# Attention and a gated MLP interleaved on TensorE: every phase takes four score units, and the slots of the other products are spread evenly over the phases

## The chip, the core and the metric

The kernel runs on one core of a Trainium2 chip. The metric is the device time in microseconds (us) of one execution, smaller is better. The times shown of the kernel before are three runs with a median of 1246.99 us (1246.35 to 1248.84).

## The reference, cut to what matters

One input x of 2048 tokens by 512 features goes through two branches, which a gate mixes token by token.

```python
g = sigmoid((x * gate_w).sum(-1, keepdims=True))
# branch A: 32 query heads of 16 features, one shared key head and value head
q = (x @ wq).reshape(B, S, 32, 16).transpose(0, 2, 1, 3)
p = softmax(einsum("bhqd,bkd->bhqk", q, x @ wk) * 16 ** -0.5)
a = einsum("bhqk,bkd->bhqd", p, x @ wv)   # heads side by side, then @ wo
# branch B: 512 -> 1792 -> 512
b = square(relu(x @ w1 + b1)) @ w2 + b2
out = g * a + (1 - g) * b
```

The weights wq and wk are drawn large, so scores are large and the kernel shifts them before the exponential by bounds on the norms of q and k. A second, exact path (`exact_shift`) stands behind a flag at the end and does not run on these inputs.

## The kernel before, in words

**Attention, in score units.** The work of branch A is cut into 32 iterations, each for four heads and 512 queries. An iteration has 16 key tiles of 128 keys, and each key tile is taken for two halves of 256 queries: 32 *score units* in an iteration, 1024 in all (`total`, L1000). `scores` (L723 to L735) makes one unit: two matmuls (L730; one on rows 0 to 63 of the array, one on rows 64 to 127, which run beside each other) fill a PSUM tile `s` of 128 keys by 1024, and ScalarE takes its exponential into `e` in SBUF (L734). The pool of `s` has two buffers (`sp`, L254), so the scores of a unit cannot be written before the exponential of the unit two places earlier has read its buffer. `context` (L737 to L747) multiplies the exponentials by the values: for two units together four matmuls of 512 columns, or for units one by one four of 256 columns (in the last iteration, where `place`, L718, orders the units by halves first), each head on its own 32 columns of the array (L745). The result gathers in `acc`.

**All other products, in slots.** Query projection, both MLP layers and the output projection are one long stream (`stream`, L188; `work`, L942). A product of 128 tokens by 512 has 12 steps or so, three for each 128 deep slice, since numbers are split into a rounded part and a rest. A step that is taken is called a *slot*: a matmul on rows 0 to 63 of the array and the partner, on rows 64 to 127, of a step taken five slots before (`LAG`, L214). So a slot issues two matmuls that run beside each other, or one alone where the stream starts, ends or has to wait for data. The variable `left` (L1001) counts the slots that are still to come; it starts at 1720. When a product is complete, VectorE takes it out of PSUM (L637 to L643 and L664 for the MLP, L239 to L242 and L972 for the output projection). The pool `mp` has three PSUM buffers.

**Phases.** The main loop (L1044 to L1058) works in phases. The order on TensorE is written by hand: `phase` (L1003) issues the scores of the next few units and, between them, slots; after it `context` handles the units of the phase before. In `phase`, the first unit's scores come first, then slots, with a further unit's scores after every third slot if the phase has more than three slots (L1020), and what is left of the units after the last slot (L1022). `plan` (L1030) says how many units and slots a phase takes:

```python
if left > max(total - u - 4, early) and u % FULL == 0:
    return range(u, min(u + FULL, total)), 8
return range(u, min(u + LIGHT, total)), 3 if left > total - u else 2
```

As long as more slots are left than units, a phase takes four units and eight slots; later phases take two units and two or three slots. In the built program that makes 175 phases of four units with eight slots each, and then 162 phases of two units with two slots each (some of these slots issue a single matmul).

**Chores.** Once in each phase `turn_of_chores` (L606) does a small piece of other work: it splits a weight tile, loads something, or splits a piece of the attention's output. It keeps a rough clock of its own, which a phase advances by 4.9 or 2.1 (L609), and a budget that depends on whether the phase has more than three slots. In phases of more than three slots the rounding of weights runs on ScalarE (L1026 to L1028, the copies of L491); in smaller phases VectorE does it (L617). `finish` (L761) copies `acc` out at the end of an iteration, on ScalarE (L771). The query norms (`qnorm`, L427) take one `s` buffer four times in the run, and the pieces of the division by the row sums run one in a phase (`side`, L1011).

**The end.** After the last unit the loop runs one phase without scores, then the last context, and then: what is left of the stream (L1064), the last half of the attention output (`half`, L818, with short filler matmuls, `busy`), and two last products.

Of the kernel before, what the change touches and what calls it, by code (L numbers as in the profile page):

```python
# [22 lines left out]
NC, CH = 4, 512  # L23
NG = 8
NK = S // 128
NF = F // 128
# [9 lines left out]
PARTS = [slice(a, min(a + 86, CH)) for a in range(0, CH, 86)]  # L36
LANDS = 8.0
GROUPS = (0, 1, 2, 3), (4, 5, 6, 7), (8, 9, 10), (11, 12, 13)
FULL, LIGHT = 4, 2
LAG = 5  # L40
HC = CH // 2

# [107 lines left out]
def mix_kernel(ctx: ExitStack, tc: tile.TileContext, xT, wkv, wq, wo, w12, b1, b2, cst, out):  # L150
# [37 lines left out]
    def stream(units, pp):  # L188

        late = []

        def follow(keep):
            if len(late) > keep:
                late.pop(0)()

        for unit in units:
            if unit is None:
                if late:  # L200
                    follow(0)
                    yield 1
                else:
                    yield 0
                continue
            terms, outs, tag = unit
            banks = [pp.tile([128, CH], F32, name=tag)]

            def product(i, half, terms=terms, outs=outs, banks=banks, tag=tag):
                if len(banks) == half:  # L210
                    banks.append(pp.tile([128, CH], F32, name=tag))
                a, b = terms[i]
                rows = slice(64 * half, 64 * half + 64)
                nc.tensor.matmul(banks[half], a[rows], b[rows], start=i == 0, stop=i == len(terms) - 1)  # L214
                if i == len(terms) - 1:
                    outs[half](banks[half])

            for i in range(len(terms)):
                late.append(lambda i=i, p=product: p(i, 1))
                product(i, 0)  # L220
                follow(LAG)
                yield 1
        while late:
            follow(0)
            yield 1
# [27 lines left out]
    with fast, tc.tile_pool(name="at", bufs=1) as at, \  # L253
# [207 lines left out]
        clock = 0.0  # L461
# [22 lines left out]
        def w_rest(half):  # L484
            n = len(ws[half])
            r, l = ws[half][n] = rounded[half][n]
            nc.vector.tensor_tensor(l, wf[half][n], r.bitcast(F32), OP.subtract)  # L487
            wanted.append(half)
# [4 lines left out]
        def w_split(half):  # L493
            if len(rounded[half]) == len(ws[half]):
                w_round(half, nc.vector.tensor_copy)
            w_rest(half)

        def w_ready(half):
            n = len(rounded[half])
            return (n == len(ws[half]) and n in since[half] and n < min(room[half], NC * NF)  # L500
                    and clock - since[half][n] > LANDS)
# [104 lines left out]
        def turn_of_chores(slots):  # L606

            nonlocal clock, held
            clock += 4.9 if slots > 3 else 2.1  # L609
            if soon:  # L610
                return soon.pop(0)()
            spare = (BUDGET if slots > 3 else BUDGET - 0.3) - (1.2 if side else 0.0)
            for half in halves():
                if len(rounded[half]) > len(ws[half]):
                    w_rest(half)
                    spare -= 0.7
                elif slots < 4 and spare > 1.0 and w_ready(half):  # L617
                    w_split(half)
                    spare -= 1.1
            if spare > 1.0 and chores and clock > held:  # L620
                if chores.pop(0)():
                    held = clock + 6.0

        def halves():
            return (0, 1) if len(ws[0]) < begun[0] + 2 else (1, 0)
# [371 lines left out]
            return pairs(r[:, cols], l[:, cols], wos[0][:, t], wos[1][:, t])  # L997

        side, lazy = [], stream(work(), mp)
        total, early = NC * NG * 2 * NK, 4 * 9 + 6  # L1000
        left = 12 * (15 + NC * NF * 2 + 3 * 4) + early + 2 * LAG  # L1001

        def phase(us, slots):  # L1003

            nonlocal left
            us = list(us)
            if ripe:
                qnorm(ripe.pop(0))
            ripe.extend(narrow)
            narrow.clear()  # L1010
            if side and next(side[0], "end") == "end":  # L1011
                side.pop(0)
            turn_of_chores(slots)
            if us:
                scores(us.pop(0))
            for i in range(1, slots + 1):
                if not next(lazy, None):
                    break
                left -= 1
                if i % 3 == 0 and us and slots > 3:  # L1020
                    scores(us.pop(0))
            for u in us:  # L1022
                scores(u)
            while wanted:
                w_load(wanted.pop(0))
            for half in halves():  # L1026
                if slots > 3 and not soon and w_ready(half):
                    w_round(half, scalar_copy)  # L1028

        def plan(u):  # L1030


            if left > max(total - u - 4, early) and u % FULL == 0:
                return range(u, min(u + FULL, total)), 8
            return range(u, min(u + LIGHT, total)), 3 if left > total - u else 2

        acc, us = None, ()
        nxt, slots = plan(0)
        phase(nxt, slots)
        v_tiles(range(9, 16), vp)  # L1040
# [3 lines left out]
        while us:  # L1044
            it, k = divmod(us[0], 2 * NK)
            if k == 0 and it + 1 < NC * NG:
                q_load(it + 1)
            nxt, slots = plan(us[-1] + 1)
            phase(nxt, slots)
            if k == 0:  # L1050
                acc = ap.tile([128, CH], F32, name="acc")
            context(acc, us)
            if us[-1] % (2 * NK) == 2 * NK - 1 and it < NC * NG - 1:
                finish(it, acc)
            if us[-1] == total - NK - 1:
                side.append(half(acc, 0))
                next(side[-1])
            us = nxt  # L1058
# [51 lines left out]
```

## Time and profile before

| what | value |
|---|---|
| median of three runs | 1246.99 us |
| span of the profiled execution, first to last instruction | 1243.9 us |
| what lies around the span (median less span) | 3.1 us |
| TensorE (PE) matmuls busy | 1233.2 us, 99% of the span |
| ScalarE (ACT) busy | 1060.3 us, 85% |
| VectorE (DVE) busy | 623.1 us, 50% |
| exponentials L734 | 1024, mean 1023 ns |

The span is counted from the first to the last instruction of one profiled execution. A matmul's start is recorded, its end is modelled, so a TensorE that reads 99% busy need not be at its peak: the spacing of the starts tells more than the busy share. PEld is the load of weights into the array, which runs ahead of the matmul and carries its waits. In brackets behind an instruction stands how long its engine was idle before it, and which instruction's end released it; "issue" means that the profile shows no wait. Consecutive exponentials overlap a little, so two of them take less than twice the duration of one.

### The profile page before, as it was taken

The page shows a single profiled execution, that of the slowest core. Times are in us where ns is not written, and L with a number is a line of the kernel's source. Part 1 is how long each engine was busy: PE and PEld are TensorE (multiplying, and loading weights), DVE is VectorE, ACT ScalarE, POOL GpSimd, SP SyncE. Part 2 cuts the span into 40 slices and gives each one's busy share as a digit, 9 for nine tenths or more (in the row PEclk, how much of TensorE's full clock was granted, in tenths as well). Part 3 has the DMA queues.
Part 4 walks back from the last instruction along what each step waited for, and adds up shares of the span by engine and source line. Part 5 has one row for each costly group of instructions (what it writes and reads, how often), then busy time and mean ns, then how long its engine had stood idle before and what let it go on. Part 6 is the DMA issues. An engine that isn't in the chain of part 4 may idle for free.

```text
span 1243.9 us, 24095 instructions
## 1 busy us (share of the span) xinstructions
PE 1233.2 (99%) x9839; PEld 612.5 (49%) x9839; DVE 623.1 (50%) x1246; ACT 1060.3 (85%) x1178; POOL 59.4 (5%) x75
## 2 busy tenths in 40 slices
PE   9999999999999999999999999999999999999997
PEld 4555555555555555555555555555433333343343
DVE  5666665545565542744827365355441454232433
ACT  6888888888888987988988888888899999999985
POOL 1000300000002000000200000002000000000000
PEclk9999999999999999999999999999999999999999
DMA  6334321211232210222202121121110120011101
GB/s 215 101 96 143 105 79 40 82 48 65 69 113 84 75 57 25 82 73 98 72 29 82 65 81 61 56 81 65 56 57 26 35 69 31 31 48 47 44 31 37
DMA packets 44388, 85.57 MB, mean 69 GB/s; under 512 B 10450, under 2 KB 10706, under 8 KB 43760
## 3 DMA queue, kind: packets, MB, share of 16 engines
q1 hardware_dynamic: 37024, 68.27, 17.0%
q0 software_dynamic: 7104, 15.44, 3.7%
q8 instruction: 79, 1.29, 0.4%
q14 instruction: 37, 0.30, 0.1%
q10 hardware_dynamic: 144, 0.26, 0.1%
HBM read 54.68 MB, written 20.97 MB: 61 GB/s over the span
## 4 chain that ended last, share of the span: by engine, by line
PE 96%; ACT 1%; DVE 1%; DMA 0%; issue 0%; SPq 0%; ACTq 0%
PE acc L745 38%; PE mm L214 31%; PE s L730 25%; ACT e L734 1%; PE mm L312 1%; DMA xf<-in_xT 0%; PE mm L186 0%; PE s L322 0%; DVE kmx L334 0%; PE acc L352 0%; ACT w1r L491 0%; PE mm L802 0%; DVE ot L1073 0%; DVE xlagain L179 0%; DVE w1l L487 0%
## 5 line engine op out<-in xcount | busy, mean ns | idle before, releaser
L734 ACT ACTIVATE e<-s 128x1024 f32<-128x1024 f32 x1024 | 980.3, 1023 | 153.5 <-PE s L730 152.0
L745 PE MATMUL acc<-e,v_ext 128*32 128x512 f32 (+1 forms) x4224 | 509.4, 587 | 0.0
L730 PE MATMUL s<-qa,k_aug 49*128 49x512 f32 x2048 | 452.6, 433 | 0.1
L730 PEld LDWEIGHTS s<-qa,k_aug 49*128 49x128 f32 x2048 | 193.7, 183 | 331.8 <-ACT e L734 300.2
L664 DVE SCALAR_TENSOR_TENSOR res<-mm,omg,res 128x512 f32<-128x512 f32 x128 | 95.8, 750 | 252.2 <-PE mm L214 252.2
L214 PE MATMUL mm<-w2r,hr 64*128 64x512 f32 x896 | 212.2, 393 | 1.0 <-DVE big L641 0.6
L745 PEld LDWEIGHTS acc<-e,v_ext 128*32 128x32 f32 x4224 | 102.7, 108 | 208.7 <-issue 202.0
L214 PE MATMUL mm<-w2l,hr 64*128 64x512 f32 x448 | 159.4, 393 | 0.0
L214 PEld LDWEIGHTS mm<-w2r,hr 64*128 64x128 f32 x896 | 129.0, 187 | 18.4 <-DVE res L664 1.2
L214 PEld LDWEIGHTS mm<-w2l,hr 64*128 64x128 f32 x448 | 83.4, 187 | 7.4
L214 PE MATMUL mm<-xragain,w1l 64*128 64x512 f32 x224 | 80.3, 393 | 0.0
L214 PE MATMUL mm<-xr,w1l 64*128 64x512 f32 x224 | 79.4, 393 | 0.0
L214 PE MATMUL mm<-xlagain,w1r 64*128 64x512 f32 x224 | 79.2, 392 | 0.0
L214 PE MATMUL mm<-xragain,w1r 64*128 64x512 f32 x224 | 78.7, 392 | 0.0
L214 PE MATMUL mm<-xl,w1r 64*128 64x512 f32 x224 | 78.5, 391 | 0.0
L214 PE MATMUL mm<-xr,w1r 64*128 64x512 f32 x224 | 77.0, 392 | 0.0
L641 DVE TENSOR_TENSOR big<-big,mm 128x512 f32<-128x512 f32 x56 | 38.5, 687 | 75.0 <-PE mm L214 74.9
L758 DVE RECIPROCAL n<-n 128x86 f32<-128x86 f32 x90 | 61.9, 688 | 3.1
L637 DVE TENSOR_SCALAR big<-mm,b1t 128x512 f32<-128x512 f32 x56 | 42.0, 750 | 39.0 <-PE mm L214 36.9
L214 PEld LDWEIGHTS mm<-xr,w1r 64*128 64x128 f32 x224 | 41.7, 186 | 4.1
L214 PEld LDWEIGHTS mm<-xragain,w1l 64*128 64x128 f32 x224 | 41.7, 186 | 3.9
L214 PEld LDWEIGHTS mm<-xl,w1r 64*128 64x128 f32 x224 | 41.7, 186 | 3.9
(160 smaller groups left out, 1136.8 us busy)
## 6 DMA issues: line engine op xcount, KB each, us to landing
stage<-in_w SPq DMA_DIRECT2D x56, 256.0 KB
qa<-qs SPq DMA_DIRECT2D x186, 64.0 KB
w1f<-in_w SPq DMA_DIRECT2D x28, 256.0 KB
w2f<-in_w SPq DMA_DIRECT2D x28, 256.0 KB
qs<-qr SPq DMA_DIRECT2D x16, 256.0 KB
ress<-res POOLq DMA_DIRECT2D x4, 1024.0 KB, 4.1
qs<-ql POOLq DMA_DIRECT2D x15, 256.0 KB, 8.2
oc<-accs SPq DMA_DIRECT2D x30, 128.0 KB
```

What stands on the lines that cost most here:

```text
L214: nc.tensor.matmul(banks[half], a[rows], b[rows], start=i == 0, stop=i == len(terms) - 1)
L312: nc.tensor.matmul(kvq[c][64 * i:64 * i + 64], wkvf[:, k], xf[c, k], start=a == 0, stop=a == 1, skip_group_check=True, tile_position=(0, 6 ...
L637: nc.vector.tensor_scalar(h[0], p, b1t[:, f:f + 1], None, op0=OP.add)
L641: nc.vector.tensor_tensor(h[0], h[0], p, OP.add)
L664: nc.vector.scalar_tensor_tensor(part, p, omg[:, s:s + 1], part, op0=OP.mult, op1=OP.add)
L730: nc.tensor.matmul(s[:, r].rearrange("p (a n) -> p a n", a=2), k_aug[rows, kt * 128:(kt + 1) * 128], qa[it][rows, :, cols], start=True, st ...
L734: nc.scalar.activation(es[u // 2][:, :, mine], s.rearrange("p r (a n) -> p (r a) n", a=2), AF.Exp, scale=SCALE)
L745: nc.tensor.matmul(acc[h * 32:(h + 1) * 32, cols], v_ext[:, kt], es[u // 2][:, h % 2 * 2 + h // 2, mine], start=(kt == 0), stop=(kt == NK ...
L758: nc.vector.reciprocal(n, n)
```

## The change

The distinction of full and light phases goes. All phases take four units. The slots that are left are divided by the phases that are left, rounded up, so 1720 slots over 256 phases give seven slots in each of 184 phases and then six in each of 72, as the built program has it. Of the slots none is left over for want of work, apart from the two of the loop's last phase without scores and three single matmuls behind the last context. The chores' clock advances by 4.6 in every phase. Since every phase with scores has more than three slots, all 112 roundings of weight tiles now stand on ScalarE (before: 97 there and 15 on VectorE). The four-unit phase is otherwise built as before: with seven slots its order is scores, three slots, scores, three slots, scores, one slot, scores, context; with six slots the last two scores stand next to each other.

```diff
-FULL, LIGHT = 4, 2
+FULL = 4
...
         def turn_of_chores(slots):
...
-            clock += 4.9 if slots > 3 else 2.1
+            clock += 4.6
...
-        total, early = NC * NG * 2 * NK, 4 * 9 + 6
-        left = 12 * (15 + NC * NF * 2 + 3 * 4) + early + 2 * LAG
+        total = NC * NG * 2 * NK
+        left = 12 * (15 + NC * NF * 2 + 3 * 4) + 4 * 9 + 6 + 2 * LAG
...
         def plan(u):
-            if left > max(total - u - 4, early) and u % FULL == 0:
-                return range(u, min(u + FULL, total)), 8
-            return range(u, min(u + LIGHT, total)), 3 if left > total - u else 2
+            phases = (total - u) // FULL
+            return range(u, min(u + FULL, total)), -(-left // phases) if phases else 2
```

## The prediction

> **What bounds the kernel now.** I read the page first, then the busy time by stage, then the timeline of single phases, because the page averages over two stages that differ.
>
> ```profile
> PE 1233.2 (99%) x9839; PEld 612.5 (49%) x9839; DVE 623.1 (50%) x1246; ACT 1060.3 (85%) x1178; POOL 59.4 (5%) x75
> PE acc L745 38%; PE mm L214 31%; PE s L730 25%; ACT e L734 1%; PE mm L312 1%; DMA xf<-in_xT 0%; PE mm L186 0%; PE s L322 0%; DVE kmx L334 0%; PE acc L352 0%; ACT w1r L491 0%; PE mm L802 0%; DVE ot L1073 0%; DVE xlagain L179 0%; DVE w1l L487 0%
> L730 PEld LDWEIGHTS s<-qa,k_aug 49*128 49x128 f32 x2048 | 193.7, 183 | 331.8 <-ACT e L734 300.2
> ```
>
> By page and chain TensorE is everything. The third row spoils that: loads of score weights sat behind an exponential again and again. How a phase is paced must come from its own instructions. Stages first (each row: window, its length, then busy us by engine, clock, DMA share, GB/s):
>
> ```profile
> 0.00:34.70 34.70, 32.40 (x163) 15.37 (x163) 19.82 (x36) 21.99 (x30) 4.74 (x13) 1.00 0.64 211
> 34.70:883.20 848.50, 847.53 (x6939) 454.23 (x6935) 464.48 (x894) 719.95 (x813) 49.19 (x52) 1.00 0.23 73
> 883.20:1231.50 348.30, 347.42 (x2708) 140.06 (x2704) 134.65 (x304) 317.54 (x335) 5.48 (x10) 1.00 0.13 43
> 1231.50:1243.90 12.40, 5.84 (x41) 2.80 (x37) 4.18 (x12) 0.81 (x2) 0.00 (x0) 0.96 0.19 69
> ```
>
> The first window holds start-up and two phases; the second 173 four-unit phases, 848.5 / 173 = 4.905 us each; the third 162 two-unit phases, 348.3 / 162 = 2.15 us each; the fourth the end. The last four-unit phase and the second light one, from the timeline (start, duration, instruction):
>
> ```profile
> 878.36 0.50 PE L730 MATMUL s<-qa,k_aug 49*128 49x512 f32 x2
> 878.69 0.39 PE L214 MATMUL mm<-xragain,w1r 64*128 64x512 f32 x1
> 878.95 3.83 ACT L734 ACTIVATE e<-s 128x1024 f32<-128x1024 f32 x4 [1.07 <-PE s L730]
> 880.33 0.41 PE L730 MATMUL s<-qa,k_aug 49*128 49x512 f32 x2
> 880.57 0.39 PE L214 MATMUL mm<-xlagain,w1r 64*128 64x512 f32 x1
> 880.80 0.39 PE L214 MATMUL mm<-xragain,w1l 64*128 64x512 f32 x1
> 880.95 0.19 PEld L730 LDWEIGHTS s<-qa,k_aug 49*128 49x128 f32 x2 [0.18 <-ACT e L734]
> 881.04 0.41 PE L730 MATMUL s<-qa,k_aug 49*128 49x512 f32 x2
> 881.38 1.93 PE L745 MATMUL acc<-e,v_ext 128*32 128x512 f32 x16
> 883.23 0.50 PE L730 MATMUL s<-qa,k_aug 49*128 49x512 f32 x2
> ...
> 886.23 0.50 PE L730 MATMUL s<-qa,k_aug 49*128 49x512 f32 x2
> 886.83 1.94 ACT L734 ACTIVATE e<-s 128x1024 f32<-128x1024 f32 x2 [1.05 <-PE s L730]
> 887.36 1.06 PE L745 MATMUL acc<-e,v_ext 128*32 128x512 f32 x8
> 888.36 0.49 PE L730 MATMUL s<-qa,k_aug 49*128 49x512 f32 x2
> ```
>
> A slot or a unit's scores takes 0.235 us of TensorE (880.33, 880.57, 880.80, 881.04). The phase lasts 883.23 - 878.36 = 4.87 us, and two clocks tell that number equally well.
>
> *TensorE's own order:* first scores, 0.33 to the first slot, ten steps of 0.235 to the fourth scores, 0.34 to the context, 1.85 of context: 4.87.
>
> *The exponentials:* the first starts 0.59 after the first scores (878.95). The fourth scores need the buffer that the second exponential reads. Two exponentials take 1.94, so it is free at 880.89; the weight load goes at 880.95, with a wait on ACT in its brackets. The context starts 0.43 later and takes 1.85. So 0.59 + 1.94 + 0.06 + 0.43 + 1.85 = 4.87. This chain holds no slot.
>
> Which of the two gives way is seen where the first exponential is late, behind two roundings and a copy of `acc`:
>
> ```profile
> 108.31 0.64 ACT L491 ACTIVATE w1r<-w1f 128x512 fp32r<-128x512 f32 x1
> 108.40 0.50 PE L730 MATMUL s<-qa,k_aug 49*128 49x512 f32 x2
> 108.83 0.60 ACT L771 ACTIVATE accs<-acc 128x512 f32<-128x512 f32 x1
> 109.31 3.78 ACT L734 ACTIVATE e<-s 128x1024 f32<-128x1024 f32 x4
> 111.31 0.18 PEld L730 LDWEIGHTS s<-qa,k_aug 49*128 49x128 f32 x2 [0.38 <-ACT e L734]
> 111.74 1.92 PE L745 MATMUL acc<-e,v_ext 128*32 128x512 f32 x16
> 113.60 0.50 PE L730 MATMUL s<-qa,k_aug 49*128 49x512 f32 x2
> ```
>
> From the first exponential to the next phase it is 113.60 - 109.31 = 4.29 us here and 883.23 - 878.95 = 4.28 above. The whole delay goes into the phase (5.20 instead of 4.87), and again the context starts 0.43 after the released load. So eight slots just fill the time that the exponentials leave, and a phase of four units is 0.59 + 4.28 = 4.87 us however few slots it holds.
>
> **The change part by part.**
>
> *Light phases become four-unit phases.* A two-unit phase has no such chain inside it: its second scores use a buffer that an exponential of the phase before has left. It lasts 888.36 - 886.23 = 2.13 us, 4.26 for four units. The same four units as one phase cost 4.87 at least, 0.61 more.
>
> *Fewer slots in the other phases.* By slots these phases should get shorter by 0.235 each. By the exponentials' chain they gain nothing: the fourth scores come up sooner in TensorE's queue and wait for the same exponential. The order of the changed program confirms that the fourth scores still stand ahead of the context and that the context waits behind them in TensorE's queue; nothing is moved past that wait. What the trace does not show is a four-unit phase with seven or six slots. Bounds: no gain at all, and the full 0.235 per slot. A light phase with two single matmuls instead of four is the nearest row:
>
> ```profile
> 1130.96 0.50 PE L730 MATMUL s<-qa,k_aug 49*128 49x512 f32 x2
> 1131.53 0.40 PE L214 MATMUL mm<-xragain,w1l 64*128 64x512 f32 x1
> 1131.64 0.19 PEld L730 LDWEIGHTS s<-qa,k_aug 49*128 49x128 f32 x2 [0.16 <-ACT e L734]
> 1132.10 1.06 PE L745 MATMUL acc<-e,v_ext 128*32 128x512 f32 x8
> 1133.09 0.50 PE L730 MATMUL s<-qa,k_aug 49*128 49x512 f32 x2
> ...
> 1135.83 3.83 ACT L734 ACTIVATE e<-s 128x1024 f32<-128x1024 f32 x4 [0.20 <-PE s L730]
> ```
>
> TensorE had less to do, the load waited for ACT, and the phase took 2.13 all the same. (The last row is the one exception there: a short phase let four exponentials run without a gap over a phase border, a catching up that a four-unit phase, with its chain inside, cannot do.) I take no gain.
>
> *The pace over all.* 254 phases follow the first two. The row above gives 4.87; the mean of 4.905 holds stalls too, some of a number that stays (four query norms). I take 4.90, nearer to the mean: 254 x 4.90 = 1244.6 us, in place of 848.5 + 348.3 = 1196.8.
>
> *Chores.* Fifteen roundings move from VectorE to ScalarE, 0.63 us each. Beside the exponentials ACT has 4.87 - 3.83 = 1.04 us free in a phase. One or two roundings fit (they overlap the last exponential); with a copy of `acc` besides, the phase above shows the price, 0.33 us. In the changed program one copy of `acc` has two roundings ahead of it, as before, so I count nothing here; if all 30 copies met two, it would be 30 x 0.33 = 10 us. VectorE has fewer pieces in a phase than before and is at half load; nothing is charged. No DMA changes its size or number.
>
> *The end.* In the last iteration four transposes of the attention's output and their waits stand ahead of the scores; together with the long first context they made 348.3 - 162 x 2.13 = 3.2 us; I keep 2.0. The last rows of before:
>
> ```profile
> 1231.52 0.50 PE L214 MATMUL mm<-wor,ol 64*128 64x512 f32 x1
> 1231.94 1.07 PE L745 MATMUL acc<-e,v_ext 128*32 128x256 f32 x16
> 1232.05 0.75 DVE L972 SCALAR_TENSOR_TENSOR ot<-mm,g,ot 128x512 f32<-128x512 f32 x1 [3.03 <-PE mm L214]
> 1233.08 0.42 DVE L822 COPY ah<-acc 128x256 f32<-128x256 f32 x1 [0.28 <-PE acc L745]
> ```
>
> The last context is for four units, 1.85 instead of 1.00. One more single matmul stands ahead of it (0.24), and three behind it, with a last L972 of 0.75 us now ahead of the copy L822 on VectorE, where it was hidden by the context: some 1.8 us later. The end is 12.4 + 0.85 + 0.24 + 1.8 = 15.3 us.
>
> *Sum.* 34.7 + 1244.6 + 2.0 + 15.3 = 1296.6 us of span, 52.7 more than 1243.9. The runs' median lies 3.1 us above that span, so I predict 1246.99 + 52.7 = 1299.7, rounded to 1300 us, 4.2% slower.
>
> *The skill against the rows.* After the last scores a context starts 0.33 to 0.34 us later instead of 0.235. The Trainium skill, "TensorEngine Tiling (Array Packing)", section "Key Properties", says that a change of tiling mode drains TensorE; scores and slots use halves of the rows, the context strips of columns, so each phase changes twice, and 256 phases instead of 337 would save drains. That speaks for the change. The rows agree that a border costs something; by this rule alone the sum would go down, which is the first rival.
>
> **The rivals.**
>
> *TensorE's order paces the phase (faster).* If the fourth scores did not wait, a phase with seven slots would take 4.90 - 0.235 = 4.665 and one with six 4.43: 182 x 4.665 + 72 x 4.43 = 1168.0 instead of 1244.6, so about 1223 us, 1.9% faster. Break-even with before needs 0.21 us less in each phase, most of what a slot is worth. For it: chain and busy share name TensorE throughout, and its own order gives 4.87 too. Against it: the wait on ACT on the fourth load, and the late phase. Chance 5%.
>
> *ScalarE's extra work collides.* If most copies of `acc` meet two roundings, 1300 + 10 = 1310. Against it: only one such meeting in the changed order. 7%.
>
> *The clock gives way.* TensorE idles 0.24 to 0.47 us more in each phase. If one phase in ten ran its 12 steps at half speed, 25 x 2.8 = 70 us, about 1370. Every window above has a clock of 1.00 except the last, where TensorE is half idle. The Trainium skill, "TensorE: Matmul & The Clock Gate", section "A second HAM failure mode: psum-queue depth-cycling", tells of a kernel whose small gaps between groups of matmuls made the clock swing; no run here shows it, though the light phases have such gaps. 2%.
>
> *The slots run dry*, so that work is left for the end: the changed order fills seven slots in 184 phases and six in 72. Under 1%.
>
> **How the numbers follow.** Forecast 86%, at 1300. Its own range: with 4.875 in a phase and half the stalls 254 x 0.025 + 3 = 9 to 10 us less; with more stalls 10 more. So 1289 to 1310, which takes in the collisions, 93%. The unknown slot price has the other end at 1223, which I leave out. Differences under 0.2% can't be told from no change. Faster 5%, same 1%, slower 94%.
>
> **What would show it.** Right: contexts 4.87 to 4.91 us apart from start to end with seven and with six slots; ahead of the fourth scores a load that waits on ACT by some 0.4 to 0.6 us; exponentials busy about 3.83 us of every phase. Wrong: contexts 4.65 apart, then 4.4; no wait on ACT at the fourth scores; a clock under 1; matmuls of L214 in a long row behind the last context.

## The result, and the profile after

The changed kernel takes 1302.91 us (median of four runs, 1300.06 to 1304.91), before takes 1247.91 (four runs, 1246.35 to 1249.19): a ratio of 1.0438, interval 1.0421 to 1.0456. The profiled execution took 1300.06 us, 1298.3 of them span.

From the page of after, the busy times, the chain of waits by engine and by line, and the loads of the score weights (busy us, mean ns | idle before them, releaser):

```profile
PE 1267.9 (98%) x9839; PEld 627.0 (48%) x9839; DVE 615.9 (47%) x1231; ACT 1062.8 (82%) x1193; POOL 58.8 (5%) x75
PE 86%; ACT 12%; issue 1%; DVE 1%; DMA 0%; ACTq 0%; SPq 0%
L730 PEld LDWEIGHTS s<-qa,k_aug 49*128 49x128 f32 x2048 | 194.1, 184 | 360.3 <-ACT e L734 335.4
```

TensorE carries out the same 9839 matmuls and still reads 98% busy, although the span grew by 54 us. The busy share shows nothing of the loss. The chain does: ACT holds 12% of it, where its exponentials held 1%.

The stages of after by busy time (window, its length, busy us by engine, clock, DMA share, GB/s): start-up with two phases, the 254 others, the end.

```profile
0.00:34.65 34.65, 32.51 (x160) 14.94 (x161) 19.82 (x36) 21.99 (x30) 4.74 (x13) 1.00 0.66 210
34.65:1283.25 1248.60, 1227.59 (x9628) 608.11 (x9624) 591.25 (x1182) 1040.46 (x1162) 54.08 (x62) 1.00 0.20 62
1283.25:1298.30 15.05, 7.80 (x61) 3.90 (x57) 4.83 (x13) 0.38 (x1) 0.00 (x0) 0.88 0.21 75
```

There is one pace from start to end, 1248.6 / 254 = 4.916 us a phase, stalls included. The timeline of after (start, duration, instruction, idle before it) for a phase with seven slots, from its first scores to the next phase's, slots left out:

```profile
320.33 0.50 PE L730 MATMUL s<-qa,k_aug 49*128 49x512 f32 x2
320.94 3.80 ACT L734 ACTIVATE e<-s 128x1024 f32<-128x1024 f32 x4 [0.55 <-PE s L730]
...
322.53 0.39 PE L214 MATMUL mm<-w2l,hr 64*128 64x512 f32 x1
322.93 0.19 PEld L730 LDWEIGHTS s<-qa,k_aug 49*128 49x128 f32 x2 [0.44 <-ACT e L734]
322.93 0.50 PE L730 MATMUL s<-qa,k_aug 49*128 49x512 f32 x2
323.36 1.92 PE L745 MATMUL acc<-e,v_ext 128*32 128x512 f32 x16
...
325.22 0.50 PE L730 MATMUL s<-qa,k_aug 49*128 49x512 f32 x2
```

And the same of a phase with six:

```profile
1112.72 0.50 PE L730 MATMUL s<-qa,k_aug 49*128 49x512 f32 x2
...
1115.32 0.19 PEld L730 LDWEIGHTS s<-qa,k_aug 49*128 49x128 f32 x2 [0.67 <-ACT e L734]
1115.32 0.50 PE L730 MATMUL s<-qa,k_aug 49*128 49x512 f32 x2 [0.23 <-ACT e L734]
1115.75 1.92 PE L745 MATMUL acc<-e,v_ext 128*32 128x512 f32 x16
1117.60 0.50 PE L730 MATMUL s<-qa,k_aug 49*128 49x512 f32 x2
```

The phases last 4.89 and 4.88 us, and the four exponentials of the first run through 3.80 of them without a gap. A slot less lengthens the wait of the fourth load by 0.23 us and shortens nothing: from the released load it is 0.43 to the context and 1.85 or 1.86 from there to the next phase in both.

The wait hides from some views. In the seven-slot phase only the load's brackets show it: the matmul of the slot before starts at 322.53, its end is modelled at 322.92, and the scores start at 322.93, so TensorE's own row shows no gap. The chain of waits follows the matmuls. Asked for these two stretches, it gives in order of time (start, us, what):

```profile
322.69 0.23 PE mm L214
322.92 0.01 issue
322.93 0.49 PE s L730
...
1113.33 1.95 ACT e L734 x2
1115.27 0.04 issue
1115.32 0.50 PE s L730 x2
```

With six slots it walks to two exponentials, with seven it stays on TensorE. So the 12% come mostly from the six-slot phases at the end of the loop (72 times 1.95 us would be 140 of 1298 us, 10.8%), and the 182 phases with seven slots are bound in the same way without being counted. This shows when each fourth load is set against the exponential whose buffer it needs, that of its phase's second unit: in 254 of the 255 phases behind the first one the load starts 0.050 to 0.052 us after that exponential's end.

### The profile page after: what moved, and what is told of

It reads as the page before. It is cut to its first block, busy times and chain, and to the rows that moved or that the text cites. A ratio compares the mean times of both kernels' runs of the same rounds, so it can differ in the third digit from the quotient of the medians.

```text
span 1298.3 us, 24136 instructions
## 1 busy us (share of the span) xinstructions
PE 1267.9 (98%) x9839; PEld 627.0 (48%) x9839; DVE 615.9 (47%) x1231; ACT 1062.8 (82%) x1193; POOL 58.8 (5%) x75
## 4 chain that ended last, share of the span: by engine, by line
PE 86%; ACT 12%; issue 1%; DVE 1%; DMA 0%; ACTq 0%; SPq 0%
PE acc L745 36%; PE s L730 25%; PE mm L214 23%; ACT e L734 11%; PE mm L312 1%; DMA xf<-in_xT 0%; ACT accs L771 0%; PE mm L186 0%; DVE most L972 0%; PE s L322 0%; DVE kmx L334 0%; PE acc L352 0%; PE mm L802 0%; DVE ot L1071 0%; ACT w1r L491 0%
## 5 line engine op out<-in xcount | busy, mean ns | idle before, releaser
L745 PE MATMUL acc<-e,v_ext 128*32 128x512 f32 (+1 forms) x4224 | 492.6, 585 | 0.0
L730 PE MATMUL s<-qa,k_aug 49*128 49x512 f32 x2048 | 463.8, 445 | 19.4 <-ACT e L734 18.2
L745 PEld LDWEIGHTS acc<-e,v_ext 128*32 128x32 f32 x4224 | 111.0, 109 | 215.0 <-issue 210.7
L214 PE MATMUL mm<-xlagain,w1r 64*128 64x512 f32 x224 | 83.1, 391 | 0.0
L214 PE MATMUL mm<-xragain,w1l 64*128 64x512 f32 x224 | 76.8, 393 | 0.0
L214 PE MATMUL mm<-xragain,w1r 64*128 64x512 f32 x224 | 75.8, 392 | 0.0
L487 DVE TENSOR_TENSOR w2l<-w2f,w2r 128x512 fp32r<-128x512 f32 x28 | 19.3, 691 | 56.0 <-ACT w2r L491 56.0
L487 DVE TENSOR_TENSOR w2l<-stage,w2r 128x512 fp32r<-128x512 f32 x28 | 19.3, 691 | 51.3 <-ACT w2r L491 51.2
```

Of the source, the lines that this page charges most:

```text
L730: nc.tensor.matmul(s[:, r].rearrange("p (a n) -> p a n", a=2), k_aug[rows, kt * 128:(kt + 1) * 128], qa[it][rows, :, cols], start=True, st ...
L745: nc.tensor.matmul(acc[h * 32:(h + 1) * 32, cols], v_ext[:, kt], es[u // 2][:, h % 2 * 2 + h // 2, mine], start=(kt == 0), stop=(kt == NK ...
```

## The experiments

Two theories stand against each other. The chain theory: a four-unit phase lasts 4.87 us, by two exponentials, a released buffer and the context, as long as its slots fit beside them. TensorE's order: every slot costs 0.235 us, and what lengthens the run lies elsewhere (chores on ScalarE, the clock, the end). Phase lengths below are medians of the spacing between the first scores of one phase and of the next, over all phases of a kind. Every ratio is against before, run on the same chip beside it.

### Half the exponentials

Without the second half of each exponential (the context reads the first half's values twice) the wait should go, and every slot should count again.

```diff
-nc.scalar.activation(es[u // 2][:, :, mine], s.rearrange("p r (a n) -> p (r a) n", a=2), AF.Exp,
+nc.scalar.activation(es[u // 2][:, :2, mine], s[:, 0].rearrange("p (a n) -> p a n", a=2), AF.Exp,
...
-                 es[u // 2][:, h % 2 * 2 + h // 2, mine], ...
+                 es[u // 2][:, h // 2, mine], ...
```

> The changed kernel with half of each exponential left out (512 of 1024 columns; the context reads the other half's values twice), so ScalarE's part of the chain is about halved and TensorE's instructions stay the same. Theory (the fourth scores of a phase wait for the second exponential): the wait goes, a phase with seven slots takes about 4.84 - 0.235 = 4.61 us and one with six 4.37, which makes about 1216 us (1208 to 1228). Rival (a phase is paced by something that TensorE does itself, as its changes between tile shapes): contexts stay 4.88 us apart, about 1300 us.

> The kernel before with the same half of each exponential left out. Theory: its phases of eight slots are held by the exponentials by only some 0.03 us, its phases of two units not at all, so it gains some 6 us: about 1241 us (1236 to 1246), and is then slower than the changed kernel with halved exponentials. Rival (ScalarE's total work, 85% busy, counts everywhere): 5% or more faster, under 1190 us.

The edited after takes 1218.40 us (1218.30 to 1218.95), 0.9774 of before (0.9758 to 0.9790); the edited before 1239.08 us, 0.9940 (0.9923 to 0.9956). Timeline of the edited after, a phase with seven slots:

```profile
302.20 0.50 PE L730 MATMUL s<-qa,k_aug 49*128 49x512 f32 x2
...
304.42 0.19 PEld L730 LDWEIGHTS s<-qa,k_aug 49*128 49x128 f32 x2
304.65 0.39 PE L730 MATMUL s<-qa,k_aug 49*128 49x512 f32 x2
304.97 1.92 PE L745 MATMUL acc<-e,v_ext 128*32 128x512 f32 x16
306.83 0.50 PE L730 MATMUL s<-qa,k_aug 49*128 49x512 f32 x2
```

The fourth load has no brackets any more and runs ahead of its matmul, and the phase lasts 4.63 us. Medians are 4.615 with seven slots and 4.407 with six: a slot counts 0.21 us once the exponentials are short. (With six slots the fourth load still waits for its halved exponential, 0.20 us in the median, which may be why the step is under 0.235; with seven and eight it doesn't.) The same edit takes 0.066 of before's time from after (1.0438 to 0.9774) and 0.006 from before, whose eight slots keep TensorE at 4.860 a phase by themselves. So the even spread would have been the faster order (1218 against 1239) with exponentials of half the size. This is the strongest evidence that the exponentials set after's pace.

### Fewer products

The third of three terms of most products is left out, in both kernels, so that 1198 slots are to be placed in place of 1720: five and four in a phase of after.

```diff
-    def pairs(ar, al, br, bl):
-        return [(ar, br), (ar, bl), (al, br)]
+    def pairs(ar, al, br, bl, n=2):
+        return [(ar, br), (ar, bl), (al, br)][:n]
...
-        left = 12 * (15 + NC * NF * 2 + 3 * 4) + 4 * 9 + 6 + 2 * LAG
+        left = 12 * 12 + 8 * (3 + NC * NF * 2 + 3 * 4) + 4 * 6 + 4 + 2 * LAG
```

> The changed kernel with about a third of the other products' matmuls left out (the third of three terms, but for most query projections), 1198 slots instead of 1720, evenly spread as five and four in a phase. Theory: a phase of four units lasts 4.88 us with any number of slots up to eight, so the time stays at 1300 us (1292 to 1304). Rival (each slot costs 0.235 us of TensorE): 522 x 0.235 = 123 us less, about 1180 us.

> The kernel before with the same third of the other products left out: 45 phases of four units with eight slots and 422 of two units with two. Theory: 43 x 4.905 + 422 x 2.15 = 1118 us in place of 1196.8, so about 1169 us (1160 to 1178). Rival (each slot costs 0.235 us wherever it stands): 123 us less, about 1125 us.

After with 30% fewer slots takes 1311.26 us (1.0508, 1.0485 to 1.0531), no less than with all of them; before takes 1183.90 (0.9496, 0.9480 to 0.9512). The same work left out saves 62 us in the one and nothing in the other. Phases of after last 4.881 with five slots and 4.879 with four. The time still lies above the expected 1292 to 1304, for other reasons, seen in its trace. Its span is 12.6 us longer than after's. Of this 3.7 fall in the start-up (38.33 us against 34.65), where 10.2 us ran at half clock, and 9.1 in the loop, where slots wait for VectorE to read a product out and two windows of 3.41 us have half clock. Shorter products come round to their PSUM buffers sooner, which would explain the stalls; it wasn't tried by itself. One of them in the timeline of the cut after, and the largest sum of them among its waits (engine, tile and line, waiting for whom: us in all, times, longest):

```profile
622.47 1.41 DVE L664 SCALAR_TENSOR_TENSOR res<-mm,omg,res 128x512 f32<-128x512 f32 x2 [2.76 <-PE mm L214]
623.28 0.50 PE L214 MATMUL mm<-w2r,hr 64*128 64x512 f32 x1 [0.62 <-DVE res L664]
```

```profile
PE mm L214 <- DVE res L664: 8.9, 15, 1.2
```

### Seven and nine slots in before

```diff
-                return range(u, min(u + FULL, total)), 8
+                return range(u, min(u + FULL, total)), 7
```

> The kernel before with one number changed, seven slots instead of eight in a phase of four units: 234 such phases and 44 of two units. Theory: a phase with seven slots lasts as long as one with eight, so 232 x 4.90 + 44 x 2.15 = 1231 us in place of 1196.8, about 1282 us (1276 to 1287). Rival (each slot costs 0.235 us): 232 x 4.67 + 95 = 1178 us, about 1229 us.

> The kernel before with nine slots instead of eight in a phase of four units: 145 such phases, five more in which the stream waits for data and gives no slot, and 212 of two units. Theory: from the ninth slot on TensorE's own order is the longer clock, 4.84 + 0.235 = 5.08 us, so 143 x 5.10 + 5 x 4.88 + 212 x 2.15 = 1209.5 us in place of 1196.8, about 1260 us (1254 to 1268). Rival (slots are free in any phase of four units): 143 x 4.90 + 24 + 456 = 1181 us, about 1231 us.

Seven slots: 1284.01 us, 1.0306 (1.0288 to 1.0323). The phase stays at 4.882, so 59 more of them are needed for the same slots, and it is they that cost. Nine slots: 1267.96 us, 1.0175 (1.0158 to 1.0191). The 142 phases that hold nine slots last 5.096, and the timeline shows the other bound taking over:

```profile
61.58 0.50 PE L730 MATMUL s<-qa,k_aug 49*128 49x512 f32 x2
...
64.24 0.19 PEld L730 LDWEIGHTS s<-qa,k_aug 49*128 49x128 f32 x2
64.80 1.92 PE L745 MATMUL acc<-e,v_ext 128*32 128x512 f32 x16
66.65 0.50 PE L730 MATMUL s<-qa,k_aug 49*128 49x512 f32 x2
```

The fourth load waits for nobody. Eight is the kink of a four-unit phase: up to it slots are free, and the ninth costs 0.215 us (5.096 against 4.881 with eight).

### Filling the wait

Matmuls that compute the third scores a second (seven slots) or third time (six slots) are put where the wait is: 328 steps of 0.235 us, 77 us of TensorE.

```diff
-                    scores(us.pop(0))
+                    scores(us.pop(0), 8 - slots if i == 6 else 0)
...
-            for r in range(2):
+            for r in [0, 1] * (1 + more):
```

> The changed kernel with useless work added: in every phase the third scores are computed twice (seven slots) or three times (six slots), so that each phase has as many steps of 0.235 us as a phase with eight slots. Theory: these steps stand in time that TensorE waits anyway, and the third exponential is not in the chain; the time stays at that of the changed kernel, 1298 to 1304 us, and the clock falls to a half less often. Rival (each step of TensorE costs): (182 + 2 x 72) x 0.235 = 77 us more, about 1378 us.

1304.45 us (1303.97 to 1304.65), 1.0461 (1.0445 to 1.0477), within 1.6 us of after; phases of 4.880 and 4.882. The 77 us of work fit into the wait. Its chain of waits reads as before's did, though the pace is after's:

```profile
PE 97%; DMA 1%; DVE 1%; ACT 0%; issue 0%; SPq 0%; ACTq 0%
```

### Context in two halves

The context of two units goes ahead of the fourth scores, so that these come later and TensorE works while it would wait.

```diff
-            phase(nxt, slots)
             if k == 0:
                 acc = ap.tile([128, CH], F32, name="acc")
-            context(acc, us)
+            phase(nxt, slots, lambda: context(acc, us[:2]))
+            context(acc, us[2:] if nxt else us)
```

> The changed kernel with the context of a phase in two parts of two units, the first ahead of the fourth scores and the second behind them, so that TensorE has work while the second exponential runs; two more changes of tile shape in each phase. Theory: no wait at the fourth scores; a phase with seven slots takes 2.45 + 0.10 + 1.00 + 0.34 + 1.00 = 4.89 us, as before, one with six 4.65, so 72 x 0.23 = 17 us less than the changed kernel, about 1286 us (1278 to 1298). Rival (TensorE's order and its changes of shape pace the phase): the two more changes come on top, about 0.25 us in each of 254 phases, 1365 us.

1308.19 us, 1.0493 (1.0476 to 1.0511): no gain, some 20 us over what I expected. The timeline, seven slots:

```profile
404.38 1.06 PE L745 MATMUL acc<-e,v_ext 128*32 128x512 f32 x8
405.37 0.19 PEld L730 LDWEIGHTS s<-qa,k_aug 49*128 49x128 f32 x2 [0.84 <-ACT e L734]
405.37 0.50 PE L730 MATMUL s<-qa,k_aug 49*128 49x512 f32 x2
405.80 1.06 PE L745 MATMUL acc<-e,v_ext 128*32 128x512 f32 x8
406.80 0.51 PE L730 MATMUL s<-qa,k_aug 49*128 49x512 f32 x2
```

The fourth scores stand between two contexts and take 0.43 us from their start to the next context's (405.37 to 405.80), not 0.235, and half a context takes 0.99 or 1.00, together 0.13 more than the 1.86 of a whole one. With seven slots the phase is 4.96, with six 4.71: slots count again (0.25 each), so the wait is gone, and the borders that were added eat what it gave. I had priced them too low. The bracket of the fourth load misleads here: the exponential whose buffer it needs ended 0.97 us before the load started (median over the phases), and the load of the next phase's first scores stands behind the same 0.84 us, with "issue" for a releaser.

### Roundings on VectorE

```diff
-                    w_round(half, scalar_copy)
+                    w_round(half, nc.vector.tensor_copy)
```

> The changed kernel with all 112 roundings of weight tiles on VectorE instead of ScalarE. Theory: ScalarE's total work does not set the time, only the stalls where two roundings meet a copy of the context's result go: 1296 to 1303 us. Rival (ScalarE is too full): 112 x 0.63 = 71 us less, about 1232 us.

1300.75 us, 1.0435 (1.0418 to 1.0453), phases of 4.882 and 4.880. All 112 roundings leave ScalarE, and the time stays. The chores on ScalarE aren't the cause.

### Four units everywhere, slots packed first

This takes the two parts of the change apart: four units in all phases, but eight slots in a phase until none is left.

```diff
-            return range(u, min(u + FULL, total)), -(-left // phases) if phases else 2
+            return range(u, min(u + FULL, total)), min(8, max(left, 0)) if phases else 2
```

> All phases of four units, but eight slots in a phase as long as the stream gives any, and then none: 213 phases with eight slots, some 40 with no slot or few. Theory: bunched or spread makes no difference, a phase of four units lasts 4.88 us with eight slots and with none: about 1303 us (1297 to 1312; the end has ten more single matmuls). In the phases without slots TensorE rests almost half the time; if the clock gives way there, up to 40 x 1 us more. Rival (the even spread itself is what costs): near the kernel before, under 1270 us.

1349.92 us (1346.84 to 1358.20), 1.0848 (1.0812 to 1.0883). The stages of its profile, then three neighbouring phases without slots:

```profile
34.70:1027.50 992.80, 991.62 (x8098) 530.61 (x8094) 540.01 (x1044) 841.81 (x950) 50.73 (x55) 1.00 0.22 70
1027.50:1335.00 307.50, 249.67 (x1588) 89.60 (x1586) 54.15 (x143) 200.07 (x214) 3.78 (x7) 0.86 0.07 25
1126.39:1131.26 4.87, 3.52 (x28) 1.09 (x24) 0.00 (x0) 3.77 (x4) 0.00 (x0) 1.00 0.00 0
1131.26:1137.81 6.55, 5.19 (x28) 1.27 (x24) 0.00 (x0) 3.77 (x4) 0.00 (x0) 0.74 0.00 1
1137.81:1144.23 6.42, 5.03 (x30) 1.27 (x26) 0.00 (x0) 3.77 (x4) 0.00 (x0) 0.76 0.00 0
```

At full clock a phase without a single slot lasts 4.87 us, the floor of the chain theory to the hundredth (eight of the stage's 35 such phases run so, 4.87 to 4.89). The others run part of their matmuls at half clock. The second stage holds 51 whole phases, from 1027.56 to 1318.77, 291.2 us; 51 x 4.87 = 248.4, and the other 43 us go with the lost clock: 24 windows of half clock, each 3.41 us long, lie in these phases, and half of their time is 41 us. So four-unit phases alone, with the slots packed as before, cost some 104 us over the 1246.22 of before beside them, and the even spread takes some 47 of these back: by the floor alone the two orders would take the same, but with six and seven slots the clock holds.

### Two units everywhere, and fewer slots in light phases

The same idea from the other side: the even spread with phases of two units, three or four slots each; and, in before, light phases with one slot, so that more phases can be light.

```diff
-FULL = 4
+FULL = 2
...
-            clock += 4.6
+            clock += 2.4
```

> Slots spread evenly as in the changed kernel, but over phases of two units: 328 phases with three slots and 184 with four. Theory: a phase of two units has no wait inside, so TensorE's order paces it and each slot counts, 2.13 + 0.235 = 2.37 us with three and 2.60 with four: 328 x 2.37 + 184 x 2.60 = 1256 us, less four phases in the start, 1246 in place of 1196.8, about 1296 us (1286 to 1304). Rival (slots are free in small phases too): 508 x 2.15 = 1092 us, about 1142 us.

```diff
-            if left > max(total - u - 4, early) and u % FULL == 0:
+            if left > max((total - u - 4) * 3 // 4, early) and u % FULL == 0:
                 return range(u, min(u + FULL, total)), 8
-            return range(u, min(u + LIGHT, total)), 3 if left > total - u else 2
+            return range(u, min(u + LIGHT, total)), 2 if left >= total - u else 1
```

> The kernel before with another mix that the theory points to: 199 phases of four units with eight slots, 106 of two units with one slot and 8 with two, that is 24 phases fewer in all. Theory: eight slots fill a phase of four units to the edge; a phase of two units with one slot is held by its two exponentials at about 1.94 us instead of 2.15: 197 x 4.905 + 106 x 1.95 + 8 x 2.15 = 1190 us in place of 1196.8, about 1240 us (1236 to 1245). Rival (a phase of two units is already held by its exponentials with two slots, 2.15 us): 197 x 4.905 + 114 x 2.15 = 1211 us, about 1260 us.

Two units everywhere: 1303.18 us, 1.0455 (1.0439 to 1.0471), with phases of 2.359 (three slots) and 2.595 (four). There each slot costs its 0.235, and each pair of units pays the borders around a context of its own. One-slot light phases: 1247.17 us, 1.0004 (0.9995 to 1.0013), where I expected 1240. Timeline of two of them in a row:

```profile
1054.93 0.50 PE L730 MATMUL s<-qa,k_aug 49*128 49x512 f32 x2
1055.62 0.18 PEld L730 LDWEIGHTS s<-qa,k_aug 49*128 49x128 f32 x2 [0.39 <-ACT e L734]
1057.05 0.50 PE L730 MATMUL s<-qa,k_aug 49*128 49x512 f32 x2
1057.53 0.19 PEld L730 LDWEIGHTS s<-qa,k_aug 49*128 49x128 f32 x2 [0.18 <-ACT e L734]
1058.95 0.50 PE L730 MATMUL s<-qa,k_aug 49*128 49x512 f32 x2
```

They last 2.12 and 1.90, 2.01 us in the mean and more beside copies of `acc`: two exponentials need some 1.9 us (3.83 for four without a gap), and the loads wait for them here too. I had taken 1.95. None of the variants that do all of the work beats before: its eight slots stand at the kink, and its light phases (2.13) not far above what two exponentials need.

## Why the prediction was right

*Step by step.* The start measured 34.65 us (34.7 predicted). The 254 phases and the last iteration's extras measured 1248.6 (1244.6 + 2.0 = 1246.6 predicted), the end 15.05 (15.3). That gives a span of 1298.3 against 1296.6. The median of the runs is 1302.9 against 1300: the runs lie 1300.06, 1302.23, 1303.59 and 1304.91 at mean clocks of 0.999, 0.998, 0.997 and 0.995, so the longer runs go with lost clock, for which the sum had no term. That the median still came within 3 us is in part luck: the sum added 3.1 us around the span, the median of before's runs less the span of another, quicker execution, while in each of these four runs the time lies 1.8 us above its own span.

*The floor of a four-unit phase.* The central step, and it held. By number of slots, all at full exponentials: 4.87 with none (at full clock), 4.879 with four, 4.881 with five, 4.879 with six, 4.883 with seven, 4.881 with eight, and 5.096 with nine. The runs with half exponentials show the reason, 4.407, 4.615 and 4.860 with six, seven and eight. Both parts are shown: taking the exponential's length away frees the phase, and adding work into the wait costs nothing.

*Light phases become four-unit phases.* The 0.61 us that the prediction put on each pair of light phases, times 81 pairs, is 49 us, most of the 55 measured. The end's longer context and products make 2.7 more (15.05 less 12.40).

*The wait by its size.* Predicted 0.4 to 0.6 us on the fourth load; the rows show 0.44 and 0.67, the medians of all phases 0.43 with seven slots and 0.66 with six.

*Chores.* Costed at nothing; with all roundings on VectorE the time is 1300.75 against 1302.91, and the two ranges overlap, so the collisions on ScalarE cost at most a microsecond or two. One of them did grow: the phase from 108.32 on, with two roundings and a copy of `acc` ahead of its first exponential, lasts 6.44 us, where before's lasted 5.20. ScalarE sat idle there for 1.14 us until the weights of the first rounding had landed, and the first exponential starts 2.17 us behind the first scores; from it to the next phase it is again 4.26. With the roundings on VectorE no phase ahead of the last iteration is longer than 5.28.

*Mis-sized.* The 2.0 us for the last iteration's extras. Its first six phases, by their first scores from 1244.85 on, last 5.25, 6.31, 5.95, 4.88, 5.59 and 5.26 us, 4.0 more than six of 4.88: the rest of the stage is 1244.6, as summed. Twice a slot waits there for VectorE besides the transposes and the context in smaller pieces. The timeline of after, at the first of them:

```profile
1250.86 0.75 DVE L972 SCALAR_TENSOR_TENSOR most<-mm,g,res 128x512 f32<-128x512 f32 x1 [3.08 <-PE mm L214]
1251.66 0.49 PE L214 MATMUL mm<-wor,orr 64*128 64x512 f32 x1 [0.84 <-DVE most L972]
```

TensorE stands for 0.84 us until VectorE has read the product before out of its buffer.

*The rivals.* TensorE's order (1223) fell: its condition, no wait on the fourth load, is met in none of after's phases that are shown. Half exponentials bring it about, at 1218; the split context does too, but at the price of a border. The clock (1370) was a real mechanism at the wrong number of slots: it takes hold with none (1350), while with six and seven the profiled execution has no half clock in the whole loop. That borders between scores and context cost time, which spoke for fewer phases, holds, and the split context shows it: the border that it adds makes up for the wait that it removes. The Trainium skill, "TensorEngine Tiling (Array Packing)", section "Key Properties", has the array drained at a change of mode; the rows agree in direction, 0.32 to 0.43 us at a border against 0.235 in a row of steps. But fewer borders, 256 phases in place of 337, were worth less than the floor of the longer phases.

## What to carry to other kernels

Where scores and exponentials pass two buffers to and fro, a phase has a floor made of exponentials, release and context, and TensorE work below that floor is free: place as much as fits up to the kink, then make the remaining phases as short as their own floor allows, instead of spreading work evenly. Whether a third buffer for the scores would lower the floor was not tried. An engine that reads 98 or 99% busy can still be waiting: look for the waits of its weight loads and count the spacing of starts, since modelled ends close the gaps and the chain of waits then stays on the wrong engine. To find out which of two equal clocks sets a phase, shorten one of them and add work to the other.

## What the hardware showed beyond that

*The clock gives way without a long pause.* In the packed variant's second stage TensorE waited for exponentials often, but never long (who waits for whom: us in all, times, longest), yet the clock was halved again and again:

```profile
PE s L730 <- ACT e L734: 54.6, 82, 1.0
```

Its timeline has the context of one phase at full clock and of the next at half:

```profile
1129.41 1.93 PE L745 MATMUL acc<-e,v_ext 128*32 128x512 f32 x16
...
1134.28 3.60 PE L745 MATMUL acc<-e,v_ext 128*32 128x512 f32 x16
```

Sixteen matmuls take 3.60 us instead of 1.93. Over that phase the granted clock is 0.74: 0.26 x 6.55 = 1.70 us lost, as if 3.4 us had run at half speed. By modelled ends TensorE was busy for 3.52 of 4.87 us in the phase before, 72%. With six slots, where the fourth load waits 0.67, the clock stayed at 1.00 over the stage. The Trainium skill, "TensorE: Matmul & The Clock Gate", section "A second HAM failure mode: psum-queue depth-cycling", tells of a kernel in which small gaps between groups of matmuls made the clock swing between full and half; these rows agree. At which share of idle time it begins isn't settled here: the runs with four and five slots lost little (0.992 to 0.997, in the profiled one mostly in the start-up), those with many phases without slots much (0.955 to 0.965).

*Work at a border costs more than work in a row.* A unit's scores take 0.235 us among slots, and 0.43 between two contexts. Why the load isn't ahead of its matmul there wasn't tried.
